# Fused landmark attention and two-layer product: the casting queue's key heads first, shorter runs of idle matmuls, and a new set of ranks

## The chip, the cores and the metric

The kernel runs on one core of a Trainium2 chip. The metric is the device time of one execution in microseconds (us). Runs of this kernel before the change took 243.25, 243.34 and 243.63 us, a median of 243.34.

A core has a matrix engine (TensorE, PE in the profile, its weight loads PEld), a vector engine (VectorE, DVE), a scalar engine (ScalarE, ACT), GpSimd (POOL) and SyncE (SP). Each runs its own list of instructions in order, and waits on semaphores for the others. SP, ACT and POOL can issue DMAs; in this kernel those issued by POOL convert float32 to bf16 on the way, and the text calls POOL's queue the casting queue.

## The reference

```python
# q, k, v: (8, 8, 576, 64) float32; p: (8, 8, 32, 64); w_in (512, 2048); w_out (2048, 512)
def sm_attn(qq, kk, vv):
    a = softmax(qq @ kk.T / sqrt(64))
    return a @ vv
p_packed = sm_attn(p, k, v)              # 32 landmarks look at 576 tokens
x = sm_attn(q, p_packed, p_packed)       # 576 tokens look at 32 landmarks
x = x.transpose(0, 2, 1, 3).reshape(4608, 512)
h = x @ w_in
g = where(h >= 1, h, where(h <= -1, 0, (h + 1)**2 / 4))
out = g @ w_out                          # (4608, 512)
```

## The kernel before, in words

Batch by batch, 8 in all, the kernel does the following. Names in code type are those of the profile's tiles.

1. Keys and queries (`k`, `q`, 96 tokens on partitions by head and chunk) are turned to `kT`, `qT`. For batches 0 and 1 PE turns them (12 transposes for four heads into a PSUM tile `tp`, line 411, and two evictions, line 219, one on DVE and one on ACT); for later batches SP issues a transposing DMA.
2. `sp` = keys by landmarks (12 matmuls for each half of four heads, line 465), `ex` = its exp on ACT (line 471), one instruction for each half. From batch 5 on the scores are taken the other way round (line 494) and turned back by a DMA.
3. `pk` = the landmarks' weighted sums of values (line 560 for batches 0 and 1, 555 later) and the sums of the exps (line 567); `ppT` is its bf16 copy, `rs` the reciprocal of the sums.
4. `s` = queries by packed landmarks (line 625), `eT` = exp, `sm` = its sums over each head's landmarks (line 653), `ln` and `rc` = their reciprocals by way of the logarithm, `A` = the normalised weights (DVE, line 667).
5. `mp` = packed landmarks by `w_in` (line 611), copied to `M` in bf16; then h = M·A (four matmuls for each of 16 slices f of the hidden layer, line 735). x itself is never formed.
6. The activation: x on ACT (line 741), t on DVE (749) or ACT (751), hT on DVE (756).
7. The output: for each 128 tokens, 16 matmuls `o` (one for each f, line 810) over hT and `w_out`, a copy `ob`, and stores. 36 such groups over two batches each (9 to a pair).

Nothing is a plain loop on the chip. Every step is a task of a planner (class Plan) that runs when the program is built: a task has a rank, its cost on each engine that could do it, the tasks it depends on, and the buffers it takes and frees. The planner goes forward in time and gives each engine the ready task that can start first; among those that can start within 0.05 us of it, the one of lowest rank. The order it arrives at is the order in which instructions are issued, so ranks and costs settle the order alone and never a wait. The ranks are the tables `L1`, `AT` (for each batch: kT, qT, sc, pk, s2, sm, M, and a step for M's quarters), `HID` (start and step of the 16 slices h of a batch) and `OUT` (start and span of each output group).

The order of the big loads is fixed by `LOADS`: k0, v0, q0 (three parts), the quarters of w_in and w_out among k1, v1, q1 and so on, all on the casting queue, at most eight outstanding. Batch 0's keys come by two ways. Heads 4 to 7 come by the casting queue, as its first load (line 302). Heads 0 to 3 come as float32 into `k_raw` by the queues of SP and ACT (line 348) and are cast by DVE and ACT, two heads each (line 219). The landmarks of batches 0 and 1 come as float32 too (`p_raw`) and are cast by DVE (`p_nat`). In the plan, the load of `k_raw` costs its queue 1.0 us and takes 4.3 us.

Before the first `o` PE has gaps. They are filled with idle matmuls on zeros (line 862, `o<-zeros`), whose number comes from the planned gap:

```python
for t in (t for t in order if t.engine == "PE"):
    if t.start >= first_o:
        break
    n = math.ceil((t.start - at) / 0.2135) if at < 5.0 else int((t.start - at - 0.1) / 0.1085)
```

A full 512-wide idle matmul counts for two, a half-wide one for one.

Of the kernel before, what the change touches and what calls it, by code (L numbers as in the profile page):

```python
# [131 lines left out]
def kernel(  # L132
# [39 lines left out]
    Q0 = [range(0, 8, 2), range(1, 5, 2), range(5, 9, 2)]  # L172
    LOADS = "k0 v0 q0 win0 win1 wout0 k1 win2 win3 wout1 v1 wout2 q1 wout3 v2 q2 p k2"
    LENT = [1, 3, 4]
    L1 = -34.393
    AT = [dict(kT=3.827, qT=-107.435, sc=47.624, pk=192.736, s2=11.248, sm=82.031, M=84.352, **{"M+": -285.897}),
          dict(kT=-1.541, qT=72.957, sc=50.923, pk=85.433, s2=8.066, sm=-2.666, M=-1.891, **{"M+": 96.506}),
          dict(kT=31.942, qT=122.067, sc=263.12, pk=148.587, s2=14.713, sm=5.141, M=-1.769, **{"M+": 12.99}),
          dict(kT=27.692, qT=303.021, sc=114.654, pk=79.143, s2=160.945, sm=10.941, M=6.893, **{"M+": 14.497}),
          dict(kT=67.873, qT=110.034, sc=205.606, pk=211.249, s2=74.773, sm=0.474, M=117.635, **{"M+": -22.797}),  # L180
          dict(kT=72.345, qT=231.89, sc=297.943, pk=504.41, s2=80.302, sm=9.342, M=89.466, **{"M+": -23.073}),
          dict(kT=427.486, qT=269.423, sc=245.881, pk=509.452, s2=-121.361, sm=34.912, M=27.096, **{"M+": 13.19}),
          dict(kT=-119.423, qT=285.0, sc=271.015, pk=10.704, s2=2.668, sm=110.422, M=80.19, **{"M+": 57.677})]
    HID = [(91.569, 0.5596), (68.62, 2.0349), (74.308, 4.6843), (198.955, 0.8354), (223.962, 12.3511), (216.239, 0.3158), (-9.911, 9.2723), (446.906, 1.443)]
    OUT = [[(299.0, 84.151), (334.967, 36.969), (128.185, 121.202), (392.136, 12.316)],
# [7 lines left out]

    V, A_, G_ = nc.vector, nc.scalar, nc.gpsimd
    nc.scalar.preload_act_table_set("natural_log_exp_and_others")
# [14 lines left out]
    plan = Plan(dict(BUFS, dma=8, exn=1))  # L210
# [52 lines left out]
    consts = plan.add(-1000, {"DVE": (2.4, 2.4, constants)})  # L263
# [80 lines left out]
    p_first = plan.add(-1000, {"SP": (1.0, 3.3, load_p_raw)})  # L344
# [2 lines left out]
        for i, queue in enumerate((nc.sync, nc.scalar)):  # L347
            queue.dma_start(k_raw[:, 2 * i:2 * i + 2], rows_of("k", 0, range(2 * i, 2 * i + 2)))

    k_first = plan.add(-999, {"SP": (1.0, 4.3, load_k_raw)}, behind=[p_first])  # L350
    casts = [plan.add(-30.2 + 0.1 * i, either(
        (0.5, 0.55), (0.8, 0.85), (lambda i=i: tokens("k", 0)[:, 2 * i:2 * i + 2], lambda i=i: k_raw[:, 2 * i:2 * i + 2])),
        [k_first], behind=landed["k", 0, 4]) for i in range(2)]
# [4 lines left out]
    pT_of, pads = {}, []  # L358
# [32 lines left out]
    def attention(b, at, fine):  # L391

        ready = {}
# [52 lines left out]
            return [t]  # L446

        users = {}
        for nm in "kq":
            parts = Q0 if (nm, b) == ("q", 0) else [range(4), range(4, 8)]  # L450
            users[nm] = [turned(nm, hs, i) for i, hs in enumerate(parts)] if b < FIRST else crossed(nm)
            plan.release(nm, users[nm])

        def scores(i):
            def mm(e):
                have["sp", b, i] = sp = wide([P, 4 * X * G, 2 * NP], f32, "sp")
                kT = have["kT", b].rearrange("p h e t -> p (h e t)")
                for c in range(E):
                    for g in range(G):
                        for a in range(2):  # L460

                            j = (G * (2 * i + a) + g) * E + c
                            w = TP if j % (4 * E) == 4 * E - 1 else P
                            o = sp[:w].rearrange("p (c x g) (a n) -> p c x g a n", x=X, g=G, a=2)[:, c, :, g, a]
                            nc.tensor.matmul(o, kT[:, j * TP:j * TP + w], pT[:, b, g, 2 * i + a],  # L465
                                             start=True, stop=True)

            def ex(e):
                if i == 0:
                    have["ex", b] = new("ex", [TP, E * X * G, Q * NP], bf16)  # L470
                nc.scalar.activation(have["ex", b][:, :, 64 * i:64 * i + 64], have["sp", b, i][:TP, :E * X * G],
                                     AF.Exp, scale=scale)

            t = plan.add(at["sc"] + 0.5 * i, {"PE": (0.39, 0.56, mm)}, ready["k", 4 * i] + pT_of[b],
                         ["w", "ex"] if i == 0 else ["w"])
            x = plan.add(at["sc"] + 0.5 * i + 0.01, {"ACT": (0.74, 0.8, ex)}, [t],
                         behind=[ready.get("ex0")])
            ready[f"ex{i}"] = x
            plan.release("w", [x])
            return t  # L480

        if b == 0:
            pads.append(plan.add(-27, {"DVE": (0.8, 0.8, lambda e: [V.memset(exn[..., TP:], 0.0), V.memset(
                pT[:, 2:TURN].rearrange("p b g a x n -> p (b g a x n)"), 0.0)])},
                                 [consts], behind=ready["k", 4]))

        def turned_scores():
            def mm(e):
                for g in range(G):
                    have["s1", b, g] = s1 = wide([P, X, FW], f32, "s1")  # L490
                    for a in range(Q):
                        for x in range(X):
                            r = slice(x * D, (x + 1) * D)
                            nc.tensor.matmul(s1[a * NP:(a + 1) * NP, x, :HALF], pT[r, b, g, a, x],
                                             have["kT", b][r, G * a + g].rearrange("p e t -> p (e t)"),
                                             start=True, stop=True)

            def ex(e, g):
                if g == 0:
                    have["ks", b] = new("ks", [P, G], f32)  # L500
                nc.scalar.activation(exn[:, g, :, :, :TP],
                                     have["s1", b, g][:, :, :HALF].rearrange("p x (e t) -> p x e t", e=E),
                                     AF.Exp, scale=scale, accum_out=have["ks", b][:, g:g + 1])

            t = plan.add(at["sc"], {"PE": (0.28, 0.43, mm)}, ready["k", 0] + pT_of[b], ["w"] * G, mode="s")
            before = None
            for g in range(G):
                ready[f"ex{g}"] = before = plan.add(
                    at["sc"] + 0.2 * g + 0.01, {"ACT": (0.8, 0.87, lambda e, g=g: ex(e, g))}, [t],
                    ["exn", "ks"] if g == 0 else [], behind=[before])  # L510
                plan.release("w", [before])
            return t
# [9 lines left out]
            return t  # L522

        turned_k = b >= TURN
        plan.release("kT", [turned_scores()] if turned_k else [scores(0), scores(1)])
        if turned_k:
            ready["exT"] = untwisted()

# [14 lines left out]
        def packed(e):  # L543
# [21 lines left out]
            for g in range(G):  # L565
                for c in range(NC):
# [3 lines left out]
        t = plan.add(at["pk"], {"PE": (0.7 if turned_k else 1.01, 0.87 if turned_k else 1.18, packed) if paired else (1.28, 1.45, packed)},  # L570
                     ([ready["exT"]] if turned_k else [ready["ex0"], ready["ex1"], consts])
                     + (pairs if paired else landed["v", b, 0]),
                     ["w", "ppT"], mode=None if paired else "pk")
# [56 lines left out]
        s2 = {}  # L630
        for gs in [[0], [1]] if fine else [[0, 1]]:
            needs = {id(t): t for g in gs for h in range(g, H, G) for t in ready["q", h]}
            t = plan.add(at["s2"] + 0.01 * gs[0], {"PE": (0.04 + 0.12 * len(gs), 0.19 + 0.12 * len(gs), lambda e, gs=gs: probs(gs))},
                         (pp if len(gs) > 1 else [pp[gs[0]]]) + list(needs.values()), ["w", "eT"] * len(gs), mode="s")
# [10 lines left out]
        for g in range(G):  # L645
# [24 lines left out]
            r = at["sm"] + 0.2 * g  # L670
# [6 lines left out]
            n = 2 if AHALF and b == 0 else 1  # L677
# [16 lines left out]
        for fs in groups:  # L694
            parts = [[0], [1]] if WPARTS and (b, fs) == (0, [0]) else [[0, 1]]
            r = at["M"] + at.get("M+", 2.0) * fs[0]
# [151 lines left out]
    order = plan.run({"PE": 0.05, "ACT": 0.05, "DVE": 0.05, "SP": 0.0, "DMA": 0.0})  # L848
    first_o = min(t.start for t in o_of.values())
    fill, at = [], 1.2  # L850
    for t in (t for t in order if t.engine == "PE"):
        if t.start >= first_o:
            break
        n = math.ceil((t.start - at) / 0.2135) if at < 5.0 else int((t.start - at - 0.1) / 0.1085)
        if n > 0:
            fill.append((at, n))
        at = t.start + t.ways["PE"][0]
# [40 lines left out]
```

## Time and profile before

| | |
|---|---|
| runs | 243.25, 243.34, 243.63 us; median 243.34 |
| profiled execution | 243.42 us; span of the trace 241.6 us |
| PE busy | 231.7 us (96% of the span), 2138 matmuls |
| ACT busy | 189.7 us (79%) |
| DVE busy | 178.4 us (74%) |
| DMA | 37.03 MB; busy without a break until some 170 us of the span |
| chain that ended last, by engine | PE 89%, DVE 5%, DMA 2%, issue 2%, ACT 1% |
| granted TensorE clock | 1.00 throughout |

The span runs from the first to the last instruction; the execution's own time has 1.82 us more around it. PE's busy time counts a matmul from its start to its modelled end, and matmuls overlap, so a mean duration of one is more than the time by which it advances the stream; in the chain, the pieces do not overlap. "Idle" before an instruction is the time in which its engine did nothing, with the instruction or DMA that ended it behind the arrow. PEq is PE's sequencer, "issue" a wait for nothing that the profile shows.

### The profile page before, as it was taken

To read this page: it belongs to the slowest core of one execution; us is meant where nothing else is said; L and a number is where in the kernel's file an instruction comes from. 1 tells how busy PE (TensorE), PEld (TensorE's weight loads), DVE (VectorE), ACT (ScalarE), POOL (GpSimd) and SP (SyncE) were. 2 spreads that over 40 slices of the span, in tenths; PEclk is the share of its full clock that TensorE was granted. 3 is DMA by queue.
4 is the path that set the end of the run, shared out by engine and by line. 5 is a ranking of instruction groups with operands and counts; after the bars stand their busy time and mean duration, and the time that the engine had idled before them with its cause. 6 is when DMAs were issued, how large, how long until landed. Compare 5 with 4: busy or idle time off the path is not lost.

```text
span 241.6 us, 5410 instructions
## 1 busy us (share of the span) xinstructions
PE 231.7 (96%) x2138; PEld 133.9 (55%) x2174; DVE 178.4 (74%) x314; ACT 189.7 (79%) x333; POOL 28.1 (12%) x42
## 2 busy tenths in 40 slices
PE   7799899999999999999999999999999999999995
PEld 2556566466554675466555554566455664566454
DVE  4448987679947879799986888699747999099400
ACT  3578998899839989999894985998889887399412
POOL 8462005000220120030030011000000000000000
DMA  7999999999999999989999999999451020310224
GB/s 162 194 206 206 207 207 203 197 236 144 146 217 180 245 180 208 159 131 240 178 170 234 235 198 158 186 117 207 103 143 46 3 68 19 88 45 1 75 72 117
DMA packets 64058, 37.03 MB, mean 153 GB/s; under 512 B 36640, under 2 KB 59552, under 8 KB 64032
## 3 DMA queue, kind: packets, MB, share of 16 engines
q0 software_dynamic: 24256, 18.25, 51.7%
q1 hardware_dynamic: 38960, 17.87, 38.1%
q10 hardware_dynamic: 816, 0.56, 0.9%
q8 instruction: 17, 0.28, 0.5%
q14 instruction: 9, 0.07, 0.1%
HBM read 37.22 MB, written 9.44 MB: 193 GB/s over the span
## 4 chain that ended last, share of the span: by engine, by line
PE 89%; DVE 5%; DMA 2%; issue 2%; ACT 1%
PE o L810 50%; PE h L735 25%; PE mp L611 3%; DMA k_raw<-in_k_dram 2%; PE o L862 2%; DVE hT L756 2%; PE pk L555 2%; PE sm L653 2%; PE s L625 1%; PE sp L465 1%; DVE M L219 1%; PE tp L411 1%; PE pk L560 1%; PE pk L567 1%; DVE kT L219 1%
## 5 line engine op out<-in xcount | busy, mean ns | idle before, releaser
L810 PE MATMUL o<-w_out_sb,hT 128*128 128x512 bf16 (+2 forms) x575 | 139.9, 367 | 2.7 <-issue 1.6
L756 DVE SCALAR_TENSOR_TENSOR hT<-t 128x576 bf16<-128x576 f32 (+1 forms) x130 | 93.3, 746 | 4.5 <-ACT t L751 2.0
L741 ACT ACTIVATE x<-h 128x576 f32<-128x576 f32 (+1 forms) x130 | 79.1, 654 | 7.3 <-PE h L735 6.4
L810 PEld LDWEIGHTS <-hT 128*128 128x128 bf16 x608 | 55.8, 98 | 51.1 <-issue 4.9
L735 PE MATMUL h<-A,M 128*128 128x288 bf16 x512 | 77.9, 286 | 0.6 <-ACT M L219 0.3
L735 PEld LDWEIGHTS <-M 128*128 128x128 bf16 x512 | 49.8, 98 | 26.6 <-issue 1.1
L749 DVE TENSOR_SCALAR t<-x 128x576 f32<-128x576 f32 (+1 forms) x74 | 33.4, 451 | 13.1 <-ACT x L741 12.7
L751 ACT ACTIVATE t<-x 128x576 f32<-128x576 f32 (+1 forms) x56 | 38.7, 690 | 0.5
L219 ACT COPY ob<-o 128x512 f32<-128x512 f32 (+2 forms) x22 | 12.1, 548 | 21.4 <-PE o L810 21.3
L219 ACT CAST M<-mp 128x1024 bf16<-128x1024 f32 (+1 forms) x19 | 18.1, 991 | 1.8 <-PE mp L611 1.8
L219 DVE CAST M<-mp 128x1024 bf16<-128x1024 f32 (+1 forms) x14 | 16.6, 1182 | 2.7 <-PE mp L611 2.5
L667 DVE SCALAR_TENSOR_TENSOR A<-eT,rs,rc 128x576 bf16<-128x576 bf16 (+1 forms) x18 | 12.9, 747 | 7.1 <-ACT rc L662 6.9
L302 POOL DMA_DIRECT2D k<-in_k_dram x8 | 6.2, 779 | 87.5 <-DMA kT<-k 70.9
L219 DVE COPY ob<-o 128x512 f32<-128x512 f32 x16 | 10.9, 686 | 5.9 <-PE o L810 5.9
L648 ACT ACTIVATE eT<-s,rs 128x576 bf16<-128x576 f32 x16 | 11.1, 739 | 3.2 <-PE s L625 3.2
L862 PE MATMUL o<-zeros 128*128 128x512 bf16 (+1 forms) x39 | 11.1, 412 | 1.4 <-DVE zeros L255 1.2
L657 ACT ACTIVATE ln<-sm 128x576 f32<-128x576 f32 x16 | 10.3, 653 | 1.0 <-PE sm L653 0.5
L611 PE MATMUL mp<-w_in_sb,ppT 64*32 64x512 bf16 x256 | 10.3, 380 | 0.4 <-DVE kT L219 0.3
L662 ACT ACTIVATE rc<-ln 128x576 f32<-128x576 f32 (+1 forms) x18 | 10.6, 631 | 0.1
L219 ACT CAST ppT<-pk 64x128 bf16<-64x128 f32 x20 | 5.2, 260 | 5.9 <-PE pk L567 4.7
L302 POOL DMA_DIRECT2D v<-in_v_dram x8 | 6.3, 792 | 25.0 <-PE pk L560 14.1
L219 DVE CAST ppT<-pk 64x128 bf16<-64x128 f32 x12 | 3.4, 286 | 7.1 <-PE pk L567 4.4
(60 smaller groups left out, 118.6 us busy)
## 6 DMA issues: line engine op xcount, KB each, us to landing
v<-in_v_dram POOLq DMA_DIRECT2D x8, 576.0 KB, 11.3
out_dram<-ob SPq DMA_DIRECT2D x23, 192.0 KB, 4.2
k<-in_k_dram POOLq DMA_DIRECT2D x7, 576.0 KB, 8.5
q<-in_q_dram POOLq DMA_DIRECT2D x7, 576.0 KB, 12.0
out_dram<-ob SPq DMA_DIRECT2D x24, 128.0 KB, 2.6
w_out_sb<-in_moe_w_out_dram POOLq DMA_DIRECT2D x4, 512.0 KB, 19.2
w_in_sb<-in_moe_w_in_dram POOLq DMA_DIRECT2D x3, 512.0 KB, 14.7
out_dram<-ob SPq DMA_DIRECT2D x23, 64.0 KB, 4.2
```

The lines of the kernel that those rows point to most:

```text
L219: i = (nc.vector.tensor_copy if e == "DVE" else nc.scalar.copy)(to, of)
L302: G_.dma_start(tokens(nm, b)[:, heads(hs)], rows_of(nm, b, hs))
L611: m = nc.tensor.matmul(have["mp", b, f][a * NP:(a + 1) * NP, g], have["ppT", b][r, g, a], w_in_sb[r, a, f * FW:(f + 1) * FW], start=True, ...
L648: nc.scalar.activation(have["eT", b, g], have["s2", b, g][:, :, :HALF], AF.Exp, scale=rs_of[b][:, g, 1:])
L667: V.scalar_tensor_tensor(have["A", b][:, g, xs], have["eT", b, g][:, xs], rs_of[b][:, g, :1], have["rc", b, g][:, xs], ALU.mult, ALU.mult)
L735: nc.tensor.matmul(have["h", b, fi][:, hf, :HALF], have["M", b][:, g, fi * P:(fi + 1) * P], have["A", b][:, g, hf], start=(g == 0), stop=( ...
L741: nc.scalar.activation(have["x", b, fi][:, hs[0]:hs[-1] + 1], have["h", b, fi][:, hs[0]:hs[-1] + 1, :HALF], AF.Prelu, bias=-1.0, alpha=0.5)
L749: V.tensor_scalar(t, x, 1.0, 0.0, ALU.add, ALU.max)
L751: nc.scalar.activation(t, x, AF.Relu, bias=1.0)
L756: V.scalar_tensor_tensor(dst, t, 1.0, t, ALU.min, ALU.mult)
L810: nc.tensor.matmul(have["o", key][:, :w], hT[:, fi, i * P:(i + 1) * P], w_out_sb[:, fi, cols], start=(fi == 0), stop=(fi == KF - 1))
L862: nc.tensor.matmul(o[:, :w], zeros[:, :P], zeros[:, :w], start=True, stop=True)
```

## The change

The program computes the same. Four things differ.

- Batch 0's halves of the keys change places: heads 4 to 7 are turned, evicted and scored before heads 0 to 3 (`halved`), and `ex` is begun by the first half done. The clearing of `exn` and the rest of `pT` stands behind the evictions of heads 0 to 3 instead of 4 to 7. Other batches keep their order.
- The planned duration of the load of `k_raw` is 5.55 us instead of 4.3.
- In the count of idle matmuls after 5 us, the planned gap is reduced by 0.4 us instead of 0.1.
- `L1`, `AT`, `HID` and `OUT` hold new numbers throughout.

```diff
-    L1 = -34.393
-    AT = [dict(kT=3.827, qT=-107.435, sc=47.624, pk=192.736, s2=11.248, sm=82.031, M=84.352, **{"M+": -285.897}),
+    L1 = 16.247
+    AT = [dict(kT=365.357, qT=-92.869, sc=-120.303, pk=232.768, s2=58.66, sm=55.18, M=-179.82, **{"M+": 29.051}),
...
-    HID = [(91.569, 0.5596), (68.62, 2.0349), (74.308, 4.6843), (198.955, 0.8354), (223.962, 12.3511), (216.239, 0.3158), (-9.911, 9.2723), (446.906, 1.443)]
-    OUT = [[(299.0, 84.151), (334.967, 36.969), (128.185, 121.202), (392.136, 12.316)],
+    HID = [(235.742, 2.1261), (59.148, 1.7968), (141.684, 6.33), (293.878, 0.8324), (312.548, 14.3092), (300.497, 2.0471), (115.102, 3.7641), (572.087, 2.0408)]
+    OUT = [[(357.277, 49.291), (365.351, 35.916), (2.236, 33.868), (405.036, 58.544)],
...
-    k_first = plan.add(-999, {"SP": (1.0, 4.3, load_k_raw)}, behind=[p_first])
+    k_first = plan.add(-999, {"SP": (1.0, 5.55, load_k_raw)}, behind=[p_first])
...
+        halved = (1, 0) if b == 0 else (0, 1)
         for nm in "kq":
-            parts = Q0 if (nm, b) == ("q", 0) else [range(4), range(4, 8)]
+            parts = Q0 if (nm, b) == ("q", 0) else [range(4 * i, 4 * i + 4) for i in halved]
...
-                if i == 0:
+                if i == halved[0]:
                     have["ex", b] = new("ex", [TP, E * X * G, Q * NP], bf16)
...
-            t = plan.add(at["sc"] + 0.5 * i, {"PE": (0.39, 0.56, mm)}, ready["k", 4 * i] + pT_of[b],
-                         ["w", "ex"] if i == 0 else ["w"])
-            x = plan.add(at["sc"] + 0.5 * i + 0.01, {"ACT": (0.74, 0.8, ex)}, [t],
-                         behind=[ready.get("ex0")])
+            r = at["sc"] + 0.5 * halved.index(i)
+            t = plan.add(r, {"PE": (0.39, 0.56, mm)}, ready["k", 4 * i] + pT_of[b],
+                         ["w", "ex"] if i == halved[0] else ["w"])
+            x = plan.add(r + 0.01, {"ACT": (0.74, 0.8, ex)}, [t],
+                         behind=[ready.get(f"ex{halved[0]}")])
...
-                                 [consts], behind=ready["k", 4]))
+                                 [consts], behind=ready["k", 0]))
...
-        plan.release("kT", [turned_scores()] if turned_k else [scores(0), scores(1)])
+        plan.release("kT", [turned_scores()] if turned_k else [scores(i) for i in halved])
...
+    SPARE = 0.4
...
-        n = math.ceil((t.start - at) / 0.2135) if at < 5.0 else int((t.start - at - 0.1) / 0.1085)
+        n = math.ceil((t.start - at) / 0.2135) if at < 5.0 else int((t.start - at - SPARE) / 0.1085)
```

More of the change, by code (lines that the diff above doesn't have):

```diff
@@ L174 @@
     LENT = [1, 3, 4]
-    L1 = -34.393
-    AT = [dict(kT=3.827, qT=-107.435, sc=47.624, pk=192.736, s2=11.248, sm=82.031, M=84.352, **{"M+": -285.897}),
[L177 to L183, printed above, removed]
@@ L184 @@
-    HID = [(91.569, 0.5596), (68.62, 2.0349), (74.308, 4.6843), (198.955, 0.8354), (223.962, 12.3511), (216.239, 0.3158), (-9.911, 9.2723), (446.906, 1.443)]
-    OUT = [[(299.0, 84.151), (334.967, 36.969), (128.185, 121.202), (392.136, 12.316)],
[7 rows of a table removed]
+    L1 = 16.247
+    AT = [dict(kT=365.357, qT=-92.869, sc=-120.303, pk=232.768, s2=58.66, sm=55.18, M=-179.82, **{"M+": 29.051}),
+          dict(kT=67.528, qT=54.112, sc=-37.809, pk=337.633, s2=-3.825, sm=-43.469, M=361.849, **{"M+": 4.329}),
+          dict(kT=303.729, qT=272.794, sc=110.742, pk=338.731, s2=136.503, sm=40.315, M=142.905, **{"M+": -10.189}),
+          dict(kT=554.617, qT=26.881, sc=193.8, pk=204.096, s2=239.931, sm=2.374, M=126.011, **{"M+": 102.74}),
+          dict(kT=50.624, qT=54.279, sc=299.708, pk=305.98, s2=362.949, sm=109.576, M=328.94, **{"M+": -62.014}),
+          dict(kT=-46.331, qT=56.631, sc=391.272, pk=565.583, s2=57.316, sm=103.186, M=139.478, **{"M+": 78.519}),
+          dict(kT=46.746, qT=221.484, sc=335.934, pk=558.147, s2=-1.879, sm=16.956, M=-7.233, **{"M+": -278.9}),
+          dict(kT=418.389, qT=345.923, sc=551.809, pk=50.768, s2=291.826, sm=156.916, M=243.095, **{"M+": 87.573})]
```

14 rows, old and new, of the table OUT are left out of this document.

## The prediction, made before the changed kernel ran

> **What bounds the kernel now.** I read the page first, for the chain that ended last.
>
> ```profile
> span 241.6 us, 5410 instructions
> PE 89%; DVE 5%; DMA 2%; issue 2%; ACT 1%
> ```
>
> TensorE (PE) carries 89% of the chain. Next I cut the span into stretches, to see where PE is not full (second pair of columns: PE's busy time and instructions).
>
> ```profile
> 0.00:21.26 21.26, 18.33 (x222) 9.65 (x226) 10.56 (x31) 12.40 (x26) 12.29 (x22) 1.00 1.12 190
> 21.26:31.30 10.04, 9.03 (x104) 6.11 (x105) 9.42 (x18) 9.55 (x18) 0.76 (x1) 1.00 1.26 206
> 31.30:60.00 28.70, 28.36 (x298) 17.07 (x302) 22.78 (x39) 26.33 (x44) 3.22 (x4) 1.00 1.22 196
> 60.00:100.00 40.00, 39.37 (x395) 22.78 (x408) 32.40 (x58) 33.20 (x58) 5.37 (x7) 1.00 1.23 191
> 100.00:140.00 40.00, 39.43 (x358) 23.15 (x350) 34.61 (x59) 34.42 (x61) 4.96 (x6) 1.00 1.19 198
> 140.00:180.00 40.00, 39.26 (x392) 21.95 (x395) 31.39 (x54) 33.10 (x64) 1.54 (x2) 1.00 1.00 163
> 180.00:223.80 43.80, 43.14 (x309) 24.84 (x300) 35.08 (x57) 36.10 (x60) 0.00 (x0) 1.00 0.14 38
> 223.80:238.70 14.90, 14.77 (x100) 8.33 (x98) 2.17 (x4) 4.41 (x10) 0.00 (x0) 1.00 0.34 88
> ```
>
> From 31.3 us PE idles 0.34 + 0.63 + 0.57 + 0.74 + 0.66 + 0.13 = 3.07 us in 207.4: a kernel bound by PE, whose end is the moment at which the dense stream begins plus a fixed amount of matmul work. Between 21.26 and 31.3 it idles 1.01 us (10.04 - 9.03), beside DVE at 9.42 and ACT at 9.55 of 10.04. Before that, part of PE's 18.33 is idle matmuls (line 862, o<-zeros). So the change can act in three ways: by starting the stream earlier, by filling the 1.01 us, and by making the 3.07 smaller or larger. The start is read from the chain in order of time.
>
> ```profile
> 6.66 0.84 ACT k L219
> 7.55 0.61 PE tp L411 x10
> 8.18 0.57 DVE kT L219
> 8.80 0.54 PE sp L465 x12
> 9.34 0.11 PE o L862
> 9.45 0.40 PE sp L465 x12
> 9.90 1.46 PE o L862 x6
> 11.36 0.87 PE pk L560 x48
> ...
> 19.05 0.49 PE o L862 x2
> 19.54 0.26 PE h L735 x2
> ```
>
> Idle matmuls stand inside the chain, ahead of pk and ahead of the first h. Something real was waiting behind them.
>
> **The swap of key heads.** It moves 12 transposes (heads 4 to 7), their two evictions, 12 score matmuls and one exp ahead of the same set for heads 0 to 3. Nothing is added or removed. What decides is which half is there first; issues and landings (last column, us from issue):
>
> ```profile
> 1.30 0.81 POOL L302 DMA_DIRECT2D k<-in_k_dram  x1 [0.86 <-POOLq L882]
> k_raw<-in_k_dram SPq DMA_DIRECT2D x1, 288.0 KB, 5.3
> k_raw<-in_k_dram ACTq DMA_DIRECT2D x1, 288.0 KB, 5.4
> k<-in_k_dram POOLq DMA_DIRECT2D x1, 288.0 KB, 6.2
> 6.49 0.56 DVE L219 CAST k<-k_raw 96x768 bf16<-96x768 f32 x1 [0.83 <-DMA k_raw<-in_k_dram]
> 7.83 0.75 POOL L318 DMA_DIRECT2D w_out_sb<-in_moe_w_out_dram  x1 [0.48 <-DMA k<-in_k_dram]
> ```
>
> From here on a row of the timeline gives start, duration, engine, line and, in brackets, the idle time before it and its releaser. The float32 heads are castable from 6.49 and cast at 7.05 (DVE) and 7.50 (ACT, 6.66 + 0.84). The casting queue's heads land at 1.30 + 6.2 = 7.50. It is a tie, and two transposes that ran at 7.10 now stand behind the wait. How soon PE picks up a landing of that queue is bounded by two rows: 0.33 us (POOL: 7.83 - 7.50) and about 0.22 for the last query part:
>
> ```profile
> L302 POOL DMA_DIRECT2D q<-in_q_dram x1: 639/639/639, 4.7 to 4.7; - x1
> q<-in_q_dram POOLq DMA_DIRECT2D x1, 144.0 KB, 9.2
> 14.16 0.30 PEld L411 LDWEIGHTS <-q 96*128 96x128 bf16 x6 [0.17 <-DMA q<-in_q_dram]
> ```
>
> That landing is 4.7 + 9.2 = 13.9, the weight load 14.16. From below the pickup is 0.05, what PE needs after a cast (7.50 to 7.55). First scores then start at (7.50 + pickup) + 12 transposes at 0.061 (0.61 / 10) = 0.73 + 0.02 + 0.57 + 0.05: 8.92 to 9.20 against 8.80. I take 0.10 us later, since the second half's transposes, evictions and scores then follow with all inputs present, and their 0.11 us of idle matmul goes. Ends: -0.05 and +0.40.
>
> The Trainium skill (DMA: Bandwidth & Descriptors, "Anatomy of one DMA — SWDGE (gpsimd) path") fits a DMA of this queue by about 2.0 us plus its bytes over 436 GB/s. For the 576 KB that are read this gives an estimate of 3.4 us, a landing at 4.7 and a swap that pays; the trace's 6.2 us, with the other loads beside it, disagrees.
>
> The sum goes by the 6.2.
>
> **Fewer idle matmuls.** Each gap is left 0.4 us instead of 0.1 of what the planner expects, so 0.3 / 0.1085 = two or three half-width matmuls fewer in each gap after 5 us: 0.2 to 0.3 us less. What this frees depends on what was ready behind them.
>
> ```profile
> 9.37 1.50 ACT L471 ACTIVATE ex<-sp 96x768 bf16<-96x768 f32 x2 [0.20 <-PE sp L465]
> v<-in_v_dram POOLq DMA_DIRECT2D x1, 576.0 KB, 8.3
> 2.11 0.79 POOL L302 DMA_DIRECT2D v<-in_v_dram  x1
> 18.85 0.95 DVE L667 SCALAR_TENSOR_TENSOR A<-eT,rs,rc 128x288 bf16<-128x288 bf16 x2
> ```
>
> pk needs both exps (10.87) and the values (2.11 + 8.3 = 10.41, with pickup under 10.75), so it could start at 10.92 and started at 11.36: 0.44 us lost. The first h needs half of A, ready at 18.85 + 0.475 = 19.33, so 19.38 against 19.54: 0.16 lost. The gap ahead of pk also shrinks in the plan, because the scores are now planned later (float32 load 5.55 instead of 4.3 us) and pk is held there by the values' load; so I expect all of 0.44 back, and of the 0.16 all. Ends: 0.2 and 0.6 together. With the swap's +0.10, the chain of batch 0 reaches its first h 0.44 + 0.16 - 0.10 = 0.50 us earlier. The last query part (13.9) does not stop this: it feeds the second half of s alone, whose exp stands on ACT behind the first ln.
>
> What is late next: the last quarter of w_in.
>
> ```profile
> 13.30 0.74 POOL L313 DMA_DIRECT2D w_in_sb<-in_moe_w_in_dram  x1 [0.30 <-DMA q<-in_q_dram]
> w_in_sb<-in_moe_w_in_dram POOLq DMA_DIRECT2D x1, 512.0 KB, 16.2
> 29.77 0.11 PEld L611 LDWEIGHTS <-ppT 64*32 64x32 bf16 x8 [0.42 <-DMA w_in_sb<-in_moe_w_in_dram]
> 31.32 1.20 PE L735 MATMUL h<-A,M 128*128 128x288 bf16 x8 [0.33 <-ACT M L219]
> ```
>
> It lands at 13.30 + 16.2 = 29.50 whatever the head does, and its M and h follow at 31.32. The 0.50 survives only as other matmuls done before 31.3, into idle time of 1.01 us. I keep 0.40. Ends: 0 and 0.5.
>
> **The clock.** Fewer idle matmuls could let PE cool. The group of the 512-wide idle matmul between 3 and 4 us (busy time, mean ns of one), and the first transposes after the longest idle:
>
> ```profile
> L862 PE MATMUL o<-zeros 128*128 128x512 bf16 x4 | 1.9, 634 | 0.0
> 7.10 0.26 PE L411 MATMUL tp<-ident,k 96*128 96x96 bf16 x2 [0.86 <-DVE k L219]
> ```
>
> PE is slow at the start, 634 ns for one; but after 0.86 us of idling the next idle matmuls of that width follow each other at 1.46 / 6 = 0.24 us, so a gap of that length did not cool it. The new gaps leave 0.4 to 0.9, so I cost them at nothing.
>
> **Ranks settled anew; planned load 5.55 us.** Neither adds an instruction; they reorder PE, ACT, DVE and SP's stores and transposes from the first gap to the end. No row shows the new order. From above, the 1.01 us before 31.3 and about a third of the 3.07 after it could go: 2.0 us gained; from below, idle could grow by the 0.33 us of the row above at several group changes, 1.3 us for four. The planned load is now near the measured 5.3 and 5.4, so the order that was laid out for a head 1.2 us too early no longer applies; the stretches with the misfit are those before 31.3. I take 0.30 us, under a third of the 1.01 there, and nothing after.
>
> **Sum.** The profiled execution took 243.42 us (span 241.6 and 1.82 around it), 0.08 above the median of 243.34. 243.42 - 0.40 - 0.30 = 242.7.
>
> **Rivals.**
> 1. No change: 243.3. The head's 0.50 is lost at w_in's landing at 29.50, and the ranks give nothing. For it: PE already waits for that load, and DVE and ACT are nearly full there. Against: PE is dense after it, so any matmul done earlier counts.
> 2. Slower: the new order lets PE run out of work after 31.3. The mechanism is a batch's h matmuls queued in PE's order before their M is evicted, as at 31.32; place: the changes of batch at 60 to 224 us; price 0.33 each. Four make 1.3, hence 243.42 - 0.40 + 1.3 = 244.3, less what the first stretch gives, 244.0. Two cancel the forecast's gain; four end slower. For it: 0.57 to 0.74 idle in each 40 us stretch is little, and a new order has more room to lose than to gain. Against: ACT and DVE have 5 to 8 us free in each of these.
> 3. More: the order also fills the rest of the 1.01 us and some of the 3.07: 243.42 - 0.40 - 1.2 = 241.8.
> 4. The casting queue's half is there well before the casts. Then both exps end one exp (0.75) earlier, at about 10.1, pk is held by the values at 10.41 to 10.75, and starts 0.2 to 0.5 before 10.92: 242.4. The landing of 7.50 speaks against it. That would be the skill's fit (DMA: Bandwidth & Descriptors).
>
> **How the numbers follow.** A change of this kernel's time shows from 0.2%, 0.49 us: faster is under 242.85, slower over 243.83. Chances: forecast 0.40 (own range 242.3 to 243.1, a tenth of it in all beyond 242.85), rival 1 0.26, rival 2 0.21, rival 3 0.08, rival 4 0.05. Faster: 0.36 + 0.08 + 0.05 = 0.49; same: 0.04 + 0.26 = 0.30; slower 0.21. The range runs from rival 3 to rival 2, 241.7 to 244.1.
>
> **What the new profile would show.** Right: the first transposes of k read the casting queue's heads and start at 7.55 to 7.83; no float32 transposes before them; pk starts near 10.9 to 11.1, held by ACT's ex and not by L862; the first h near 19.0; PE's busy share from 21.26 to 31.3 above 9.03. Wrong: pk at 11.3 or later; a longer wait for w_in near 29.5; PE idle in the stretches after 60 us well above 0.6 in 40, by waits for M, hT or A.

## The result and the profile after

The changed kernel is slower: a median of 246.64 us over 9 runs (244.39 to 249.09) against 243.64 (243.25 to 244.30, 9 runs), a ratio of 1.0092 with a 95% interval of 1.0063 to 1.0121. Ratios here compare executions within 1.5% of a kernel's fastest; medians and ranges are over all executions. The spread is the first thing to see: 1.05 us before, 4.7 after. The profiled execution took 246.53 us (span 244.8).

From its page, the span, the granted clock in 40 slices and the chain by engine:

```profile
span 244.8 us, 5408 instructions
PEclk9979999999999999999999999999999999999999
PE 66%; DMA 12%; DVE 10%; ACT 6%; issue 2%; SPq 1%; ACTq 1%
```

PE's part of the chain fell from 89% to 66%, and 12% are now DMAs. The clock has a dip (a 7) that the page of before did not show. The same stretches as before:

```profile
21.26:31.30 10.04, 9.20 (x106) 6.25 (x108) 9.74 (x19) 9.82 (x19) 0.76 (x1) 1.00 1.26 206
31.30:60.00 28.70, 28.02 (x294) 16.74 (x297) 22.66 (x38) 25.43 (x44) 3.22 (x4) 1.00 1.21 190
60.00:100.00 40.00, 38.27 (x389) 21.97 (x401) 31.43 (x54) 32.22 (x58) 5.38 (x7) 1.00 1.24 179
100.00:140.00 40.00, 39.00 (x350) 22.48 (x341) 32.81 (x55) 33.88 (x60) 5.13 (x6) 1.00 1.17 195
140.00:180.00 40.00, 39.02 (x356) 21.70 (x368) 32.16 (x55) 33.53 (x65) 1.54 (x2) 1.00 1.01 169
```

Up to 31.3 us PE shows a little more busy time than before, in part at half the clock (below). From there to 180 us its idle time reads 0.68 + 1.73 + 1.00 + 0.98 = 4.39 us, where it read 2.28. Neither sum is all idle. The two traces hold 36 matmuls fewer than weight loads (2127 to 2163, and 2138 to 2174), and each matmul that is missing leaves a short hole that reads as idle. `b_ob6`, a run of section 3 below with the order of before, lacks none:

```profile
PE 231.7 (96%) x2138; PEld 133.9 (55%) x2174; DVE 178.4 (74%) x314; ACT 189.7 (79%) x333; POOL 28.1 (12%) x42
PE 235.8 (97%) x2174; PEld 133.7 (55%) x2174; DVE 178.7 (74%) x314; ACT 190.1 (78%) x333; POOL 28.2 (12%) x42
```

The first line is before, the second `b_ob6`. In the second, PE idles 0.28 us from 31.3 to 238.7 us. So before had next to nothing to gain there, and what counts is the difference of the two sums, about 2.1 us. Three places deserve a look.

**The head: a lead, then the clock.** PE's rows of the timeline:

```profile
7.12 1.20 PE L411 MATMUL tp<-ident,k 96*128 96x96 bf16 x24
10.59 0.94 PE L562 MATMUL pk<-ex,v 96*64 96x32 bf16 x48 [0.33 <-ACT ex L472]
13.20 0.32 PE L627 MATMUL s<-qT,ppT 64*32 64x288 bf16 x8 [0.38 <-DVE qT L219]
14.38 0.67 PE L655 MATMUL sm<-eT,onesblk 128*128 128x288 bf16 x2 [0.24 <-ACT eT L650]
16.97 0.41 PE L655 MATMUL sm<-eT,onesblk 128*128 128x288 bf16 x2
19.17 0.60 PE L737 MATMUL h<-A,M 128*128 128x288 bf16 x2
```

pk starts 0.70 us sooner than in the same view of before (11.29), held by ex as it should be. The lead is 0.69 at the first s (13.89 before) and at the first sm (15.07), and gone at the second sm, 16.97 against 16.85 before. Between them two matmuls of sm took 0.67 us, and 0.41 later. The first h is 0.21 us ahead (19.38 before). PE alone, in single microseconds (busy time and instructions, granted clock, DMA share, GB/s):

```profile
12.00:13.00 1.00, 0.81 (x18) 1.00 1.26 204
13.00:14.00 1.00, 0.81 (x14) 0.74 1.26 208
14.00:15.00 1.00, 0.76 (x12) 0.50 1.23 209
15.00:16.00 1.00, 1.00 (x11) 0.50 1.26 206
16.00:17.00 1.00, 1.00 (x4) 0.55 1.23 206
17.00:18.00 1.00, 1.00 (x13) 1.00 1.24 204
```

The clock was halved from about 13.5 to 16.9 us, though no idle stretch of PE there was longer than 0.4 us.

**Batch 3's keys.** PE's longest wait after 31 us is this one, for keys that a DMA turns (the first two lines are of the changed kernel, the third of before):

```profile
PE sp L466 <- DMA kT<-k: 1.0, 1, 1.0
69.61 9.55 SPq L440 DMA_TRANSPOSE kT<-k  x1
69.58 8.17 SPq L440 DMA_TRANSPOSE kT<-k  x1
```

The scores start at 86.07, when the keys have landed, 16.4 us after the DMA was issued. Before, the same DMA took 12.8 us, and PE did not wait.

**The middle: copies that wait for stores.** One output copy, SP's queue and POOL's loads around 120 us, then the chain there:

```profile
112.29 0.68 DVE L219 COPY ob<-o 128x512 f32<-128x512 f32 x1
116.23 5.52 SPq L440 DMA_TRANSPOSE kT<-k  x1
121.86 3.79 SPq L440 DMA_TRANSPOSE qT<-q  x1
125.75 8.50 SPq L831 DMA_DIRECT2D out_dram<-ob  x10
125.85 0.77 POOL L302 DMA_DIRECT2D k<-in_k_dram  x1 [16.40 <-DMA kT<-k]
126.61 0.77 POOL L302 DMA_DIRECT2D v<-in_v_dram  x1
```

```profile
126.34 6.08 DMA out_dram<-ob
...
132.52 0.59 ACT ob L219
...
133.16 0.81 PE o L812 x3
```

SP's two transposing DMAs hold it for 9.4 us, and the stores behind them leave only at 125.75, together with the next batch's loads. The second part of the store of the copy made at 112.29 goes out at 126.3 and lands at 132.4. There are four `ob` buffers; the fourth copy after that one (120.11, 126.74, 127.18, 132.52) stands on ACT, with everything queued behind it. From the waits after 31 us:

```profile
ACT ob L219 <- DMA out_dram<-ob: 3.1, 1, 3.1
PE o L812 <- ACT ob L219: 0.6, 1, 0.6
```

ACT stands for 3.1 us, but PE, which has other work in its order, waits 0.6 us for that copy.

Before, the same place has this:

```profile
122.72 9.89 SPq L829 DMA_DIRECT2D out_dram<-ob  x10
out_dram<-ob SPq DMA_DIRECT2D x1, 64.0 KB, 4.8
130.89 0.59 ACT L219 COPY ob<-o 128x512 f32<-128x512 f32 x1 [2.30 <-PE o L810]
DMA to landing us min/median/max: 3.3/6.4/7.1
```

The second line is the second part of the store that this copy needs, issued at 123.3: it lands at 128.1, 2.8 us before the copy, which waits for PE alone. The last line has all stores issued from 110 to 140 us; their landing varies by more than those 2.8 us.

How much each place cost is read against `a_ob6` (section 3), whose trace has the same order of work and none of the three. The changed kernel's matmuls come 0.69 us later than there at 28 us, 0.5 at 65, 1.7 at 86, 1.9 at 113, 2.6 at 133 and 2.95 from 149 us to the end. The largest step is the wait for batch 3's keys, 1.2 us. The clock makes the first 0.7, of which 0.5 are left at 65 us; the copy's wait makes 0.7, and another wait for turned keys 0.3 at 149 us.

### The profile page after: what moved, and what is told of

It is laid out like the page before. It is cut to its first block, busy times and chain, and to the rows that moved or that the text cites. A ratio compares the mean times of both kernels' runs of the same rounds, so it can differ in the third digit from the quotient of the medians.

```text
span 244.8 us, 5408 instructions
## 1 busy us (share of the span) xinstructions
PE 233.1 (95%) x2127; PEld 133.9 (55%) x2163; DVE 178.4 (73%) x307; ACT 192.5 (79%) x340; POOL 28.8 (12%) x42
## 4 chain that ended last, share of the span: by engine, by line
PE 66%; DMA 12%; DVE 10%; ACT 6%; issue 2%; SPq 1%; ACTq 1%
PE o L812 36%; PE h L737 16%; DMA kT<-k 10%; DVE hT L758 7%; PE o L865 4%; PE mp L613 3%; DMA out_dram<-ob 2%; DVE t L751 2%; ACT x L743 2%; ACT t L753 2%; PE sm L655 2%; PE s L627 1%; PE pk L557 1%; PE tp L411 1%; ACT ex L472 1%
## 5 line engine op out<-in xcount | busy, mean ns | idle before, releaser
L753 ACT ACTIVATE t<-x 128x576 f32<-128x576 f32 (+1 forms) x63 | 42.7, 685 | 0.7
L751 DVE TENSOR_SCALAR t<-x 128x576 f32<-128x576 f32 (+1 forms) x67 | 30.4, 453 | 8.4 <-ACT x L743 8.3
L219 ACT COPY ob<-o 128x512 f32<-128x512 f32 (+2 forms) x20 | 10.9, 545 | 18.5 <-PE o L812 15.4
L219 DVE CAST M<-mp 128x1024 bf16<-128x1024 f32 (+1 forms) x16 | 19.0, 1187 | 4.3 <-PE mp L613 4.3
L669 DVE SCALAR_TENSOR_TENSOR A<-eT,rs,rc 128x576 bf16<-128x576 bf16 (+1 forms) x18 | 12.8, 747 | 6.3 <-ACT rc L664 6.2
L219 ACT CAST M<-mp 128x1024 bf16<-128x1024 f32 (+1 forms) x17 | 16.0, 988 | 1.0 <-PE mp L613 1.0
L219 DVE COPY ob<-o 128x512 f32<-128x512 f32 x18 | 12.3, 686 | 5.8 <-PE o L812 5.8
L865 PE MATMUL o<-zeros 128*128 128x512 bf16 (+1 forms) x29 | 10.2, 500 | 1.2 <-DVE zeros L255 1.2
L219 ACT CAST ppT<-pk 64x128 bf16<-64x128 f32 x24 | 6.2, 260 | 5.5 <-PE pk L569 4.8
L472 ACT ACTIVATE ex<-sp 96x768 bf16<-96x768 f32 x10 | 7.7, 808 | 1.0 <-PE sp L466 1.0
```

The lines of the kernel that those rows point to most:

```text
L219: i = (nc.vector.tensor_copy if e == "DVE" else nc.scalar.copy)(to, of)
L669: V.scalar_tensor_tensor(have["A", b][:, g, xs], have["eT", b, g][:, xs], rs_of[b][:, g, :1], have["rc", b, g][:, xs], ALU.mult, ALU.mult)
L751: V.tensor_scalar(t, x, 1.0, 0.0, ALU.add, ALU.max)
L753: nc.scalar.activation(t, x, AF.Relu, bias=1.0)
L865: nc.tensor.matmul(o[:, :w], zeros[:, :P], zeros[:, :w], start=True, stop=True)
```

## The experiments

Each kernel is compared with executions of the kernel before on the same chip. The four groups ran on four chips, so kernels of two groups are compared by their ratios to before. Where an order is kept, the instructions of every engine, idle matmuls aside, stand in the order of the parent.

**1. Each part by itself.** `b_gaps`: before with `- 0.1` changed to `- 0.4` in the count of idle matmuls. `a_gaps`: the changed kernel with `SPARE = 0.1`. `b_swap` and `a_unswap` exchange the steps of the two halves after planning:

```diff
+    for key in [k_ for k_ in swp if k_[-1] == 0]:
+        t0, t1 = swp[key], swp[key[:-1] + (1,)]
+        t0.start, t1.start, t0.engine, t1.engine = t1.start, t0.start, t1.engine, t0.engine
+    order = sorted(order, key=lambda t: t.start)
```

> The kernel before, with only the rule for idle matmuls changed (0.4 us spared in each gap instead of 0.1); its order of real work is untouched. Theory C (the clock: the shorter runs of idle matmuls let PE's granted clock fall to half for a few us, as the changed kernel's trace shows from 13.5 to 16.9 us): granted clock under 1.00 in the same place, 0.5 to 1.0 us slower than before, about 244.3. Theory O (all of the loss is the new order of work): clock drop or not, within 0.3 us of before. My prediction as it stands on record (no cooling, overruns freed): up to 0.4 us faster, 243.0.

> The changed kernel, with only the rule for idle matmuls put back (0.1 us spared); its order of real work is untouched. Theory C: clock 1.00 throughout, and the 3 us come back: about 243.3. Theory O: clock 1.00, only 0.5 to 1.0 us come back, about 245.6, with the wait for batch 3's turned keys near 86 us and the idle PE after 60 us still there, and the times still spread over more than 1 us.

> The kernel before, with only the swap of batch 0's key halves: the planner runs as before, and then the two halves' steps change places in the order (turning, evictions, scores, exps). Ranks, planned costs and idle matmuls are those of before. If the swap is a tie, as predicted: within 0.2 us of before, and k's first transposes at 7.1 to 7.8. Theory S (the casting queue's half comes late and costs): 0.3 us or more slower. If it comes early: 0.3 us faster, unless the idle matmuls ahead of pk hide it, which the start of ex shows.

> The changed kernel's ranks alone: idle matmuls by the old rule (0.1 us) and the halves of batch 0's keys exchanged back, by changing their places in the changed kernel's order. Theory O: as slow as the changed kernel with the old rule for idle matmuls, within 0.5 us of it, 245 to 246, and spread over more than 1 us. Theory S or C alone: within 0.5 us of the kernel before.

| | ratio to before, 95% | median, range (us) | clock 0.993 or less |
|---|---|---|---|
| b_gaps | 1.0030, 1.0008 to 1.0051 | 244.56, 243.66 to 245.98 | 2 of 12 |
| a_gaps | 1.0003, 0.9981 to 1.0025 | 243.85, 243.08 to 247.79 | 1 of 12 |
| b_swap | 1.0002, 0.9981 to 1.0023 | 244.00, 243.01 to 245.33 | 1 of 12 |
| a_unswap | 1.0022, 0.9997 to 1.0048 | 244.36, 242.99 to 246.03 | 0 of 12 |

The swap is a tie. The new ranks without the new gaps (`a_unswap`, and `a_gaps` with the swap) are not clearly slower than before, against what theory O expected; `a_gaps` came back to the time of before, as theory C expected. 5 of 12 and 3 of 12 of their executions took over 245 us, where 4 of 35 of the kernel before did, whose slowest took 247.40. The new gaps cost 0.3% in the old order, where a gain was expected, and the clock was 0.998 or more in 10 of 12 executions; what costs the 0.3% was not found. Why the lead in the head brings nothing there, PE's rows of `b_gaps` show:

```profile
10.49 0.94 PE L560 MATMUL pk<-ex,v 96*64 96x32 bf16 x48
18.57 0.65 PE L735 MATMUL h<-A,M 128*128 128x288 bf16 x4
29.71 0.41 PE L611 MATMUL mp<-w_in_sb,ppT 64*32 64x512 bf16 x8 [0.66 <-DMA w_in_sb<-in_moe_w_in_dram]
31.26 0.96 PE L735 MATMUL h<-A,M 128*128 128x288 bf16 x6 [0.32 <-ACT M L219]
```

pk and the first h are 0.8 us ahead of before (11.29, 19.38). About half of that is no merit of the gaps: in this execution ex began at 8.90 instead of 9.37, its loads having landed sooner. At the last quarter of w_in PE waits 0.66, and the next h starts at 31.26 instead of 31.32.

**2. Which gap, and the price of the clock.** `a_again` is the changed kernel unaltered. `a_pkshort` and `a_pklong` give the new rule to the gap ahead of batch 0's pk only, or to all others only. `b_nofill` counts no idle matmul after 5 us (`if n > 0 and at < 5.0`).

> The changed kernel itself, unaltered, beside the others on this chip. Theory C (the clock): again 0.5 to 1.0% slower than before, with a mean granted clock near 0.993 (half speed for some 3.4 us) in about half of its executions or more, where before has that in 1 of 35. Theory O (order): slower by as much in the executions at clock 1.00 as in those at 0.993.

> The changed kernel with the old rule for idle matmuls (0.1 us spared) in every gap but the one ahead of batch 0's pk, which keeps the new rule's 0.4 us. If any gap before 21 us will do to lose the clock, or the one ahead of pk does it: clock 0.993 in several executions and 0.5% slower. If it is the idle PE between 12 and 15 us (ahead of s and sm): clock 1.00 and 0.3 to 0.5 us faster than before, 243.4 or less where before is 243.9, since pk starts 0.4 us sooner.

> The changed kernel with the old rule in the gap ahead of pk alone and the new rule in all others. The reverse of the one above: if the gap ahead of pk decides, clock 1.00 and the time of before; if those between 12 and 15 us do, clock 0.993 in several executions and 0.5% slower than before.

> The kernel before with no idle matmuls at all after 5 us (30 to 40 fewer); its order of real work is untouched. It measures the price of the clock by itself. Theory C: clock 0.993 or below in nearly every execution, one or more stretches at 0.50 before 25 us, 1 to 2 us slower than before. If idle matmuls are dead weight, as my prediction costed them: clock 1.00 and 0.4 us faster than before.

| | ratio to before, 95% | median, range (us) | clock 0.993 or less |
|---|---|---|---|
| a_again | 1.0080, 1.0048 to 1.0111 | 245.72, 243.80 to 247.03 | 1 of 6 |
| a_pkshort | 1.0032, 1.0005 to 1.0058 | 244.45, 243.38 to 247.20 | 2 of 12 |
| a_pklong | 1.0024, 0.9997 to 1.0052 | 244.30, 243.03 to 250.97 | 3 of 13 |
| b_nofill | 1.0107, 1.0073 to 1.0140 | 247.21, 244.53 to 249.66 | 7 of 7 |

`a_pkshort` and `a_pklong` lie between before and the changed kernel, with intervals that just overlap its own: neither gap alone decides, and each loses the clock in a few executions, so that neither expectation came out as it stood. The clock is real: without idle matmuls it was lost in every execution (0.969 to 0.979). In the profiled one it fell at 12 us and was still low past 20:

```profile
12.00:13.00 1.00, 1.00 (x16) 0.50 1.28 203
19.00:20.00 1.00, 0.53 (x3) 0.50 1.24 205
21.26:31.30 10.04, 9.47 (x91) 0.79 1.26 206
```

But it does not explain the result: in the second comparison four of the six executions had the clock at 1.00, and three of those still took 245.61 to 245.75 us. The slowest execution of `a_pklong`, 250.97 us, was the one profiled. ACT's longest wait for a DMA in it, what that cost PE, the chain and PE's stretch there:

```profile
ACT ob L220 <- DMA out_dram<-ob: 6.6, 1, 6.6
PE o L815 <- ACT ob L220: 4.0, 1, 4.0
126.67 8.38 DMA out_dram<-ob
100.00:140.00 40.00, 35.37 (x284) 0.93 1.22 191
```

The store took 8.4 us, ACT stood for 6.6, PE for 4.0, and the clock fell to 0.50 at 134.4 us, within that wait. Here the wait came before the loss of the clock, and not the reverse. `a_pkshort`'s profiled execution (244.96 us, clock 1.00) has the same wait, smaller:

```profile
ACT ob L220 <- DMA out_dram<-ob: 3.8, 1, 3.8
PE o L815 <- ACT ob L220: 1.2, 1, 1.2
```

In `a_again` the fastest of the six (243.80) was profiled: there only one copy waited for a store, for 1.0 us and at another place (88.53), and PE had no wait over 0.3 us after 31 us. None of its five slower executions has a trace.

**3. More buffers for the copies.** The planner still counts four, so the order is the same; six are allocated.

```diff
-        return work.tile(shape, dtype, tag=tag, name=tag, bufs=BUFS[tag])
+        return work.tile(shape, dtype, tag=tag, name=tag, bufs=6 if tag == "ob" else BUFS[tag])
-    p_raw = work.tile([NP, 2, H, D], f32, tag="k1", name="p_raw", bufs=1)
+    p_raw = work.tile([NP, 2, H, D], f32, tag="vv", name="p_raw", bufs=BUFS["vv"])
```

> The changed kernel with six buffers for output copies instead of four (the order of every engine is unchanged; room is made by letting the first landmarks share the place of later pair values). Theory B (the new order leaves no slack between an output copy on ACT and the store that frees its buffer; when that store takes 6 to 8 us beside the key, value and query loads near 126 us, ACT, then DVE and PE stand): the tail above 246 us goes, the median falls from 245.7 to about 244.0. Theory C (the clock before 21 us is the cause): 245.5 or more, as without the buffers.

> The changed kernel with the old rule for idle matmuls and six output buffers. Theory B: narrow, 243.0 to 243.8, no execution above 245; faster than before by up to 0.3%. Theory C: the same as without the buffers, a median at that of before and single executions above 245.

> The changed kernel with the old rule for idle matmuls in all gaps but the one ahead of pk, and six output buffers. If what the shorter run ahead of pk brings (pk 0.4 us sooner) reaches the end once the store's wait is gone: 242.9 to 243.4, the fastest of these. If not: as the kernel with the old rule everywhere and six buffers.

> The kernel before with six output buffers, as a control. Theory B: no change beyond 0.2%, since its trace shows no copy that waits for a store. If buffers help every order alike: 0.3% or more faster.

| | ratio to before, 95% | median, range (us) | without the buffers |
|---|---|---|---|
| a_ob6 | 1.0007, 0.9982 to 1.0031 | 244.33, 243.06 to 244.89 | 1.0080 |
| a_gaps_ob6 | 0.9980, 0.9959 to 1.0001 | 243.42, 243.05 to 243.91 | 1.0003 |
| a_pkshort_ob6 | 0.9979, 0.9957 to 1.0002 | 243.11, 242.98 to 243.95 | 1.0032 |
| b_ob6 | 0.9993, 0.9972 to 1.0015 | 243.88, 243.50 to 244.78 | 1 |

The changed kernel's loss goes from 0.80% to 0.07%, intervals apart, and the range from 3.2 us to 1.8; the two are from different chips, each against before on its own. By the medians 0.49 us are left (before took 243.84 on this chip). No execution of the four is above 245 us, as theory B expected. The old order gains nothing, and `a_pkshort_ob6` is no faster than `a_gaps_ob6`. In `a_ob6` the copy that had waited at 132.52 for a DMA waits for PE, as before:

```profile
129.81 0.58 ACT L219 COPY ob<-o 128x512 f32<-128x512 f32 x1 [2.29 <-PE o L812]
```

This row is no proof by itself, since `a_again`, with four buffers, has the like at 130.17; the proof lies in the times.

**4. The reverse, the clock without the stores, and the old ranks.** `b_ob3` gives before three buffers (`bufs=3 if tag == "ob"`). `b_nofill_ob6` is `b_nofill` with six. `b_swap_short_ob6` is `b_swap` with six and 0.7 us spared ahead of pk alone.

> The kernel before with three buffers for output copies instead of four, the order of every engine unchanged: the reverse of adding buffers, in the old order of work. Theory B (copies that wait for stores): the tail and the loss of the changed kernel appear here without any change of ranks or idle matmuls: 1% or more slower than before, executions spread over more than 2 us, and copies in the trace that wait for the store's landing. If the new order's fault is another (the transposes, the clock): within 0.3% of before.

> The kernel before without idle matmuls after 5 us, with six output buffers. It parts the price of the clock from the price of waiting stores, which the first kernel without idle matmuls (1.1% slower, up to 249.7) may have mixed. If that loss is the clock's: still 0.8 to 1.2% slower, clock 0.97 to 0.98. If half of it was waits for stores: about 0.5% slower and a narrow spread.

> The old ranks with the swap of the key halves, a shorter run of idle matmuls ahead of pk alone (0.7 us spared there, 0.1 elsewhere) and six output buffers. If the new ranks gave nothing and the 0.4 us at pk is all there was to gain: as fast as the new ranks with the same two things (243.1, 0.2% under before). If the new ranks are worth something once no copy waits: 243.5 or more.

`b_ob3`: 1.0096 (1.0071 to 1.0121), 245.34 to 250.44. The old order, old ranks and old gaps with one buffer less lose what the change lost, as theory B expected, with the clock at 1.00 in the profiled execution and these waits of DVE, ACT and PE:

```profile
DVE ob L219 <- DMA out_dram<-ob: 2.9, 1, 2.9
ACT ob L219 <- DMA out_dram<-ob: 2.0, 2, 1.0
PE o L810 <- DVE ob L219: 1.3, 1, 1.3
```

`b_nofill_ob6`: 1.0132 (1.0099 to 1.0165). Buffers don't mend the loss of the clock, which lasted 13.7 and 10.2 us in the two profiled executions; its price is that of `b_nofill`, including what comes later. Part of that is the wait for batch 3's keys, which here stands in the old order and with six buffers, so it belongs neither to the new ranks nor to the copies:

```profile
PE sp L465 <- DMA kT<-k: 1.1, 1, 1.1
```

`b_swap_short_ob6`: 1.0008 (0.9992 to 1.0023), 243.28 to 245.15. The swap and the shorter run give nothing with the old ranks. Beside 0.9979 for `a_pkshort_ob6`, this speaks for the new ranks being worth some 0.2 to 0.3% once no copy waits; the two were taken on different chips and their intervals overlap, so it is not settled. On one chip, `a_gaps_ob6` (0.9980) and `b_ob6` (0.9993) differ by 0.13%, with overlapping intervals too.

The fastest version is `a_pkshort_ob6`, 0.21% under before with an interval that just reaches no change, and about 1% under the changed kernel by the two ratios to before (0.9979 to 1.0080).

## Why the prediction was wrong, by its steps

The forecast was 242.7 us in a range from 241.7 to 244.1; the changed kernel took 246.64.

**Ranks settled anew** is the step that failed, and with it the sum that added it to **Fewer idle matmuls** as if the two did not touch. It took 0.30 us of gain, and its end on the side of a loss was bounded by the one stall that the trace of before showed on PE (0.33 us at an M). The runs show no such gain, and PE's wait at an M did not grow (0.3 us). With the old gaps the new ranks took as long as before (1.0003 with the swap, 1.0022 without, both intervals reaching 1). With the new gaps they lost 0.8 to 0.9%, where the new gaps lose 0.3% in the old order. Most of that loss goes with two more buffers for output copies (1.0080 to 1.0007), and before loses as much with one buffer less (1.0096). So the order's price was slack in the ring of output copies. The step asked whether PE would lack input, and not which resource had slack to lose. The rows were there: stores that take 3.3 to 7.1 us, four buffers, SP held for 9.9 us by two transposes, and 2.8 us between a landing and the copy that needs its buffer. Rival 2 had the sign, but its mechanism (h ahead of its M) was another; it was given 0.21.

Two things limit this. In the profiled execution the copy's wait is 0.7 us of the loss, less than the 1.2 us of the wait for batch 3's keys, and no trace tells which of the waits the other slow executions had. And with six buffers the new gaps still stand 0.27% behind the old ones (1.0007 and 0.9980), as in the old order (1.0030); the intervals overlap, and the cause of this part is open.

What feeds both waits in the profile is, by the order of their times, lateness of the transposing DMAs. The one of 69.61 landed at 69.61 + 16.41 = 86.0 in the changed kernel and at about 82.4 before. The next load of k, which in the program waits for a turned buffer, followed at 87.11 instead of 83.48 (the profile names no releaser there), and two batches later SP's transposes ended at 125.65 instead of 122.62. In `a_gaps`, with the same order of work, they ended at 120.5 and no copy waited; in `a_again` at 124.1, and the copy there did not wait either. So whether a copy waits turns on a few microseconds of DMA timing, which differ from one execution to the next. Why the new gaps make the late case so much more frequent (1.0080 against 1.0003 in the same order) was not found; the clock accounts for a part of the executions only. Why one transpose takes 16.4 us in one execution and 12.8 in another is open too.

**The clock** was costed at nothing, from one gap of 0.86 us that did not cool PE. The profiled execution lost 3.4 us of full clock, in 6 of 9 runs the mean was 0.993. In `a_again`, the same program, it was 1 of 6. Many short gaps were lengthened at once, and a single gap was the wrong row to judge by. Its price in the profile is some 0.6 us: the h after w_in's last quarter starts at 31.76, where `a_again` at clock 1.00 has it at 31.20 and before at 31.32.

**Fewer idle matmuls.** Right on the mechanism at pk: it is held by ex and no longer by line 862. From the start of the exps to pk it was 9.37 to 11.29, and is 9.04 to 10.59: 0.37 us saved for 0.44 expected. The other 0.33 of pk's lead is luck of this execution, whose loads landed sooner (the first cast runs at 5.76 us instead of 6.49). The 0.44 and the 0.16 at the first h were read from starts in the chain, where a piece begins only when the one before it ends. In the timeline pk started at 11.29 and that h at 19.38, just when its A was ready, so nothing was to be had at h. The time did not follow the lead: the new gaps alone make before slower (1.0030), which the ends of 0 to 0.5 us of gain did not allow.

**What is late next.** The place was named (w_in at 29.50), the amount was wrong: 0.40 of 0.50 was to be kept. `b_gaps` kept 0.06 of 0.81 past that point. That is the lower end, and rival 1's mechanism. The 1.01 and 3.07 us of idle time that were to be filled were less than they seemed: `b_ob6`, with every matmul in its trace, has 0.86 and 0.28.

**The swap** was a tie, as predicted (`b_swap` 1.0002). The pickup of 0.05 to 0.33 us was about 0.02: the load landed at 1.30 + 5.8 = 7.10 and PE began at 7.12.

## What to carry to other kernels

Before reordering work, list the waits that are nearly there: for each ring of buffers, how long after a landing its next user comes, set against how much that landing varies. An order that is as good on paper can spend that slack; with it more of the executions here were late even where the median held (8 of 24 over 245 us without the new gaps, 4 of 35 before). Before idle time is counted as room to gain, set the number of matmuls in a trace against that of weight loads. Idle matmuls that look like dead weight may be what keeps the clock. Cutting only the run that held pk back brought nothing that could be measured here (0.9979 beside 0.9980), so a cut that is right on paper is to be measured too.

## What the runs showed of the hardware

- The granted clock fell to 0.50 for 3.4 us in a stretch where PE's busy share was 0.67 to 1.00 in every microsecond from 8 us on and its longest idle was 0.4 us. Much of the work there was light (32-column matmuls and transposes). The same program kept the clock at 0.999 or more in 5 of 6 executions of `a_again`. Without idle matmuls after 5 us it fell in 13 of 13 executions, and in the kernel before in 2 of 113.
- Stores of 16 to 192 KB took 1.6 to 8.6 us to land in one and the same execution of the changed kernel, with a median of 2.8; those issued from 110 to 140 us, beside loads of the casting queue, had a median of 7.6.
- A transposing DMA of keys held SP's queue for 3.7 to 10.4 us in the kernel before.
- The kernel before gives 242.9 to 247.4 us in 122 executions, with medians from 243.5 to 243.9 on the chips of the experiments.
